# A layer's matrix products set between the small products that join the blocks of an inverse

## The chip, the cores and the metric

The kernel runs on one core of a Trainium2 chip. The metric is the device time of one execution in microseconds (us). TensorE is PE in what follows (PEld is its loading of weights), VectorE is DVE, ScalarE is ACT, GpSimd is POOL, SyncE is SP.

## The reference

A recurrence over 768 steps for 4 x 8 heads of size 40, whose output is the input of two feed-forward layers:

```python
for t in range(S):                      # S = 768, state is D x D, D = 40, for each batch and head
    y[:, :, t] = einsum('bhd,bhde->bhe', rt, state)
    Sa = einsum('bhde,bhe->bhd', state, at)
    state = state * wt[:, :, None, :] - einsum('bhd,bhe->bhde', Sa, bt) + einsum('bhd,bhe->bhde', vt, kt)
x = y.transpose(0, 2, 1, 3).reshape(3072, 320)
h = x @ w_in                            # 320 -> 1024
sm = softmax(h);  solu = h * sm         # the sum has 1e-09 added
x = layernorm(solu) * g_ln @ w_out      # 1024 -> 320
h = x @ w2_in                           # 320 -> 2048
out = (max(h, 0) + alpha * min(h, 0)) @ w2_out
```

## The kernel before

The recurrence is computed in chunks of 32 steps. There are 24 slots, `slot(g)`, one for each chunk, and 12 windows of two slots. Within a chunk the steps depend on each other through a triangular matrix of 32 x 32 for each head, whose inverse is needed. The inverses of two windows are built together, by `inverse(W)`: on DVE by 14 elimination steps for the 16 x 16 blocks, then on PE by `left` (tile pv, twice 64 matrix products) and `join` (tile pn, twice 64), which join the 16 x 16 blocks to 32 x 32. ACT copies the results (L386, L392). Each of these products is a block of 16 or 32 rows for one of four groups of partitions; `units` issues four of them for each l and then calls `pace`.

The joins for W = 1 to 5 are run in the slots 3, 7, 11, 15 and 19, at four places of the slot by `invs(0.2)`, `invs(0.4)`, `invs(0.6)` and `invs(1.0)`. The join for W = 0 is run ahead of the slots.

Within a slot PE makes, in this order: px (L437), pu (L450), pf (L473), pst (L485), pg2 (L528), pss (L505, L508) and py (L548). px needs the scans H and F of DVE (L277, L281), and py is the slot's output, multiplied by H into Yt (L552) and passed on. Before py the tile YS is copied by ACT (L535) and masked by POOL (L536).

While the recurrence runs, PE also makes the first layer for earlier chunks. For each slot `mlp_tasks` puts its work into `queue` as entries with a planned time: 16 of h (mm1, L583, one product of 128x512 each), four of ptr (tr1, L622, transposes), eight of po (mm2, L636 to L638, three products each), one of ptx (tr2, L650), and the norm (L600) and the softmax (`soft`, L588 to L597, whose power on POOL is L596). The order of PE's work is decided as the kernel is written out, by a plan of the time: `pace(dt, n)` notes the work just issued, and where the columns counted over the last 3.413 us of the plan are below a floor it calls `pop`, which issues the next entry of the queue. Where the queue is empty, `pop` issues a product whose result nobody reads: "busy" (L211) in the first slots, "zero" (L182) later, if `more()` allows it. `wait` fills planned waits the same way. Ahead of py the queue is emptied down to two entries.

The order on DVE, ACT and POOL is made by a scheduler from the same program. From about 775 us on, the second layer runs (L1022, L1040 to L1042, with L603, L604 and L1028, L1029 on the other engines).

Of the kernel before, what the change touches and what calls it, by code (L numbers as in the profile page):

```python
# [46 lines left out]
def tile_kernel(ctx: ExitStack, tc: tile.TileContext, w_fm, a0_fm, a_fm, kb_fm, r_fm, v_fm, v_tm,  # L47
# [112 lines left out]
    queue, now, seen = [], [0.0], []  # L160

    def note(dt, n):
        now[0] += dt
        seen.append((now[0] - dt, now[0], n))
        while seen[0][1] < now[0] - SPAN:
            seen.pop(0)

    def counted(ahead=0.0):
        t = now[0] + ahead - SPAN
        return sum(n * min(1.0, max(0.0, b - t) / max(b - a, 1e-6)) for a, b, n in seen)  # L170

    def pop():
        if queue:
            dt, n, f = queue.pop(0)
            f()
        elif "busy" in st:
            dt, n = 0.216, 512
            keep(1)
        else:
            dt, n = 0.216, 416  # L180
            z = ps_at.tile([128, 512], F32, name="zero", tag="at")
            nc.tensor.matmul(z, lhsT=D1[:, 1:65].bitcast(BF16), rhs=D1[:, 0:256].bitcast(BF16), start=True, stop=True)  # L182
        note(dt, n)
        return dt

    def more():
        return queue or "busy" in st or st["slot"] >= KEND and ZF[st["slot"] % 4]

    def pace(dt, n):

        note(dt, n)
        floor, extra = LEVELS[min(st["slot"] // 4, 1) if st["slot"] != 4 else 2] if st["slot"] < NG - 4 else LEVELS[3]
        if more() and counted(dt + 0.09) + n < floor:
            note(0.09, 0)
            while more() and counted() < floor + extra:
                pop()
# [12 lines left out]
    def keep(n):  # L209
        for _ in range(n):  # L210
            nc.tensor.matmul(st["busy"], lhsT=busy[:, 0:128], rhs=busy, start=True, stop=True)  # L211
# [133 lines left out]
    def inverse(W):  # L345
        X = LMN[W % 2]
        L = X[:, 0:16, :].rearrange("p t (b a) -> p b t a", b=2)
        A = LMN[2]
        box = {}

        def start():
            nc.vector.transpose(out=X[:, 15::-1, :], in_=GR[:, :, 32:48].rearrange("p l c -> p c l"))
            nc.vector.transpose(out=X[:, ::-1, 16:32].rearrange("p s c -> p c s"),
                                in_=GR[:, :, 16:32].rearrange("p l c -> p c l"))

        def step(s):
            sh = [128, 2, 15 - s, s]
            tmp = b1.tile([128, 128], F32, name="tmp")[:, 0:2 * s * (15 - s)]
            tmp = tmp.rearrange("p (b t a) -> p b t a", b=2, a=s)
            nc.vector.tensor_tensor(out=tmp, in0=L[:, :, s + 1:16, s:s + 1].to_broadcast(sh),  # L360
                                    in1=L[:, :, s:s + 1, 0:s].to_broadcast(sh), op=ALU.mult)
            o = L[:, :, s + 1:16, 0:s]
            st["step"] = nc.vector.tensor_tensor(out=o, in0=o, in1=tmp, op=ALU.add)

        def fin():
            V = b1.tile([128, 32, 16], F32, name="V", tag="Yt")
            low = tri[:, 0:256].rearrange("p (t a) -> p t a", a=16).unsqueeze(1).to_broadcast([128, 2, 16, 16])
            nc.vector.tensor_tensor(out=V.rearrange("p (b t) a -> p b t a", b=2), in0=L, in1=low, op=ALU.mult)
            nc.vector.memset(V.rearrange("p (b t) a -> p b (t a)", b=2)[:, :, ::17], 1.0)
            st["fence"] = nc.vector.transpose(out=VT.rearrange("p l a -> p a l"), in_=V.rearrange("p x a -> p a x"))  # L370
            nc.scalar.activation(out=VR[:, :, 31:15:-1], in_=VT, func=AF.Identity, scale=tri[:, 320:321])

        def units(p, lhsT, rhs, rows, ls):
            for l in ls:
                for q in range(0, 128, 32):
                    nc.tensor.matmul(p[q:q + 32, l - ls[0], :], lhsT=lhsT[q:q + rows, l, 0:32], rhs=rhs[q:q + rows, l, :],  # L376
                                     start=True, stop=True)
                pace(0.042, 16)

        def left(h):  # L380
            if h == 0:
                box["p"] = ps_at.tile([128, 32, 16], F32, name="pv", tag="at")
            p = box["p"]
            units(p[:, 16 * h:16 * h + 16], GR, VT, 16, range(16 * h, 16 * h + 16))
            if h:
                nc.scalar.copy(out=A[:, :, 0:16], in_=p)  # L386

        def join(h):
            ls = range(16 * h, 16 * h + 16)
            p = ps_at.tile([128, 16, 32], F32, name="pn", tag="at")  # L390
            units(p, A, VR, 32, ls)
            nc.scalar.copy(out=X[:, 16 * h:16 * h + 16, :], in_=p)  # L392
            st["NT", W] = X

        yield start
        for s in range(1, 15):
            yield lambda s=s: step(s)
        yield fin
        for f in (left, join):
            for h in range(2):  # L400
                yield lambda f=f, h=h: f(h)
# [396 lines left out]
    def inv_tasks(g):  # L798
        W, c4 = divmod(g, 4)
        if 2 * W + 3 >= NW or c4 < 2:  # L800
            return []
        inv = list(inverse(W + 1))
        return inv[:16] if c4 == 2 else inv[16:]
# [117 lines left out]
    def phase1():  # L921
# [19 lines left out]
        if NW > 2:  # L941
            prep_load(2)
            load_a(4)
            load_a(5)
            kb_load(2)
        inv = list(inverse(0))
        st["joins"] = inv[16:]
        for i, f in enumerate(inv[:16]):
# [416 lines left out]
```

## Time and profile before

| | |
|---|---|
| median of 3 runs | 1168.07 us |
| lowest and highest | 1164.89 and 1177.03 us |
| the profiled execution | 1169.15 us |
| its span, first to last instruction | 1167.4 us |
| mean granted clock of TensorE in it | 0.912 of full speed |
| PE busy | 1018.2 us, 87% of the span |

The profiled execution is one execution on the same core; its time is 1.75 us longer than its span. Times of the trace are counted from the span's start. Idle time of an engine is put down to what it waited for last; "issue" means that it waited for nothing that the profile shows.

### The profile page before, as it was taken

The page shows a single profiled execution, that of the slowest core. Times are in us where ns is not written, and L with a number is a line of the kernel's source. Part 1 is how long each engine was busy: PE and PEld are TensorE (multiplying, and loading weights), DVE is VectorE, ACT ScalarE, POOL GpSimd, SP SyncE. Part 2 cuts the span into 40 slices and gives each one's busy share as a digit, 9 for nine tenths or more (in the row PEclk, how much of TensorE's full clock was granted, in tenths as well). Part 3 has the DMA queues.
Part 4 walks back from the last instruction along what each step waited for, and adds up shares of the span by engine and source line. Part 5 has one row for each costly group of instructions (what it writes and reads, how often), then busy time and mean ns, then how long its engine had stood idle before and what let it go on. Part 6 is the DMA issues. An engine that isn't in the chain of part 4 may idle for free.

```text
span 1167.4 us, 43026 instructions
## 1 busy us (share of the span) xinstructions
PE 1018.2 (87%) x19030; PEld 844.2 (72%) x19030; DVE 698.0 (60%) x1382; ACT 536.1 (46%) x1222; POOL 484.2 (41%) x495
## 2 busy tenths in 40 slices
PE   7678777888887888797788889989999999999997
PEld 3455455676766776675667677778998889999997
DVE  8887876668686846584667725656534433344443
ACT  3456543666456645665565556656312121212121
POOL 6576535342353335331733233346233333333333
PEclk9799868888889967988789888999999999999999
DMA  7534343353334333342233433444401010201000
GB/s 167 142 113 113 90 129 102 81 138 101 85 92 115 104 87 94 94 126 77 64 99 92 116 107 94 117 130 143 122 4 59 10 60 10 63 6 41 6 23 15
DMA packets 104709, 100.06 MB, mean 86 GB/s; under 512 B 38084, under 2 KB 83908, under 8 KB 104516
## 3 DMA queue, kind: packets, MB, share of 16 engines
q1 hardware_dynamic: 104516, 97.24, 30.4%
q8 instruction: 151, 2.47, 0.9%
q14 instruction: 42, 0.34, 0.1%
HBM read 71.78 MB, written 25.43 MB: 83 GB/s over the span
## 4 chain that ended last, share of the span: by engine, by line
PE 49%; DVE 23%; ACT 8%; POOL 8%; issue 6%; DMA 5%; SPq 0%; POOLq 0%; DVEq 0%; ACTq 0%
PE ph L1022 15%; PE acc L1042 5%; PE acc L1040 5%; PE acc L1041 5%; PE h L583 4%; DMA kbf<-in_kb_fm_dram 3%; DVE VUS L490 2%; POOL sm L596 2%; DVE H L277 2%; DVE P L590 2%; PE busy L211 2%; DVE KBS L516 2%; DVE F L281 2%; PE pf L473 2%; PE pv L376 1%
## 5 line engine op out<-in xcount | busy, mean ns | idle before, releaser
L1029 POOL TENSOR_TENSOR gll<-gt,gh 128x512 fp32r<-128x512 f32 (+1 forms) x112 | 129.0, 1152 | 224.1 <-ACT gh L1028 223.0
L603 DVE TENSOR_SCALAR gt<-ph,al 128x512 f32<-128x512 f32 (+1 forms) x112 | 75.5, 674 | 189.7 <-PE ph L1022 189.6
L1028 ACT CAST gh<-gt 128x512 fp32r<-128x512 f32 (+1 forms) x112 | 62.5, 559 | 254.6 <-DVE gt L604 217.4
L583 PE MATMUL h<-w1h,xt 128*128 128x512 f32 x240 | 104.7, 485 | 4.4 <-ACT h L592 2.3
L536 POOL TENSOR_TENSOR YS<-YS,mask 64x512 f32<-64x512 f32 x48 | 64.3, 1340 | 84.3 <-ACT YS L535 82.6
L312 POOL TENSOR_TENSOR XS<-XS,H 40x512 f32<-40x512 f32 (+1 forms) x48 | 62.5, 1306 | 66.1 <-DMA XS<-in_a_fm_dram 32.9
L1041 PE MATMUL acc<-w2l,gh 128*128 128x320 f32 x288 | 89.0, 309 | 0.0
L1040 PE MATMUL acc<-w2h,gh 128*128 128x320 f32 x288 | 89.0, 309 | 0.0
L1042 PE MATMUL acc<-w2h,gll 128*128 128x320 f32 x288 | 88.9, 309 | 0.0
L628 DVE TENSOR_TENSOR lnl<-ptr,lnh 128x512 fp32r<-128x512 f32 x48 | 32.6, 685 | 80.3 <-ACT lnh L627 80.2
L636 PE MATMUL po<-wo1h,lnh 128*128 128x320 f32 x192 | 69.0, 359 | 8.4 <-DVE lnl L628 6.7
L211 PE MATMUL busy<-busy 128*128 128x512 bf16 x241 | 70.3, 444 | 2.3 <-POOL lims L127 1.3
L604 DVE SCALAR_TENSOR_TENSOR gt<-ph,gt 128x512 f32<-128x512 f32 (+1 forms) x112 | 68.8, 615 | 3.7
L583 PE MATMUL h<-w1l,xt 128*128 128x512 f32 x144 | 68.9, 479 | 0.0
L589 ACT ACTIVATE P<-h,sm 128x1024 f32<-128x1024 f32 x24 | 26.8, 1115 | 85.3 <-DVE sm L588 85.3
L637 PE MATMUL po<-wo1l,lnh 128*128 128x320 f32 x192 | 63.1, 329 | 2.0 <-issue 2.0
L638 PE MATMUL po<-wo1h,lnl 128*128 128x320 f32 x192 | 62.9, 328 | 0.0
L583 PEld LDWEIGHTS h<-w1h,xt 128*128 128x128 f32 x240 | 50.1, 221 | 12.8 <-ACT h L592 3.3
L1022 PE MATMUL ph<-w1h,w2h 128*128 128x512 f32 x180 | 59.3, 394 | 0.0
L336 DVE TENSOR_TENSOR XS<-pg,mask 32x256 f32<-32x256 f32 x96 | 39.8, 415 | 31.7 <-ACT GR L339 28.3
L1040 PEld LDWEIGHTS acc<-w2h,gh 128*128 128x128 f32 x288 | 54.2, 188 | 1.5
L1041 PEld LDWEIGHTS acc<-w2l,gh 128*128 128x128 f32 x288 | 54.1, 188 | 1.2
(208 smaller groups left out, 2742.0 us busy)
## 6 DMA issues: line engine op xcount, KB each, us to landing
kbf<-in_kb_fm_dram SPq DMA_DIRECT2D x24, 416.0 KB
x2d<-x SPq DMA_DIRECT2D x24, 320.0 KB
xd<-Y SPq DMA_DIRECT2D x24, 256.0 KB
xt<-xd SPq DMA_DIRECT2D x12, 512.0 KB
raw<-in_w_in_dram SPq DMA_DIRECT2D x20, 256.0 KB
wt<-in_w_fm_dram SPq DMA_DIRECT2D x24, 211.7 KB
raw<-in_w_in_dram SPq DMA_DIRECT2D x8, 512.0 KB
raw<-in_w_out_dram SPq DMA_DIRECT2D x16, 256.0 KB
```

The costliest lines, as they stand in the source:

```text
L211: nc.tensor.matmul(st["busy"], lhsT=busy[:, 0:128], rhs=busy, start=True, stop=True)
L536: nc.gpsimd.tensor_tensor(out=y[q, e], in0=y[q, e], in1=mask[q].unsqueeze(1).to_broadcast([64, 16, 32]), op=ALU.mult)
L583: nc.tensor.matmul(st["h"][:, ns], lhsT=l, rhs=r, start=j == 0, stop=j == len(ops) - 1)
L603: nc.vector.tensor_scalar(out=tmp, in0=h, scalar1=0.0, scalar2=al, op0=ALU.min, op1=ALU.mult)
L604: nc.vector.scalar_tensor_tensor(out=o, in0=h, scalar=0.0, in1=tmp, op0=ALU.max, op1=ALU.add)
L636: nc.tensor.matmul(po, lhsT=lh[:, k], rhs=wo1h[:, k], start=k == 0, stop=False)
L637: nc.tensor.matmul(po, lhsT=lh[:, k], rhs=wo1l[:, k], start=False, stop=False)
L1022: nc.tensor.matmul(p, lhsT=l, rhs=r, start=j == 0, stop=j == len(ops) - 1)
L1029: nc.gpsimd.tensor_tensor(out=gll, in0=t, in1=f32(gh), op=ALU.subtract)
L1040: nc.tensor.matmul(acc, lhsT=gh[:, cs], rhs=oh, start=f == 0, stop=False)
L1041: nc.tensor.matmul(acc, lhsT=gh[:, cs], rhs=ol, start=False, stop=False)
L1042: nc.tensor.matmul(acc, lhsT=gll[:, cs], rhs=oh, start=False, stop=f == K2 - 1)
```

## The change

In `units`, after every fourth l (that is after 16 small products) one entry of the queue is issued, if the queue holds any. Nothing else is edited. Lines of the kernel from L379 on have a number two higher afterwards.

```diff
@@ -376,6 +376,8 @@
                     nc.tensor.matmul(p[q:q + 32, l - ls[0], :], lhsT=lhsT[q:q + rows, l, 0:32], rhs=rhs[q:q + rows, l, :],
                                      start=True, stop=True)
                 pace(0.042, 16)
+                if queue and l % 4 == 3:
+                    pop()
 
         def left(h):
             if h == 0:
```

On PE, the first `left` of slot 11 and what follows it, before (pu and pv are of the recurrence and the inverse, h and ptr of the layer, pf of the recurrence again):

```order
L450 MATMUL pu<-XP,LMN_160 32x40 x32
L376 MATMUL pv<-VT,GR 32x16 x64
L459 LDWEIGHTS D_148
L459 MATMUL pf<-D_148 32x256
L473 MATMUL pf<-LMN_160,XP 40x32 x4
L583 MATMUL h<-w1h,xt 128x512
L583 MATMUL h<-w1l,xt 128x512
L583 MATMUL h<-w1h,xt 128x512
L622 MATMUL ptr<-ident,P 128x128 x2
```

The same place of PE after the change:

```order
L452 MATMUL pu<-XP,LMN_160 32x40 x32
L376 MATMUL pv<-VT,GR 32x16 x16
L585 MATMUL h<-w1h,xt 128x512
L376 MATMUL pv<-VT,GR 32x16 x16
L585 MATMUL h<-w1l,xt 128x512
L376 MATMUL pv<-VT,GR 32x16 x16
L585 MATMUL h<-w1h,xt 128x512
L376 MATMUL pv<-VT,GR 32x16 x16
L624 MATMUL ptr<-ident,P 128x128 x2
L461 LDWEIGHTS D_148
L461 MATMUL pf<-D_148 32x256
L475 MATMUL pf<-LMN_160,XP 40x32 x6
```

Three products of h and the first pair of ptr now stand between the four parts of pv, and no longer behind the first products of pf. The second `left` (pv) of the slot takes in two pairs of ptr and two products of h in the same way, and the two `join` (pn) take in seven of the eight groups of po.

The end of slot 11 on PE before, from the second join to the next slot's px:

```order
L376 MATMUL pn<-VR,LMN_162 32x32 x64
L505 MATMUL pss<-ident,VUS_167 40x40 x26
L636 MATMUL po<-wo1h,lnh 128x320
...
L638 MATMUL po<-wo1h,lnl 128x320
L182 LDWEIGHTS D_148
L182 MATMUL zero<-D_148 128x512
L505 MATMUL pss<-ident,VUS_167 40x40 x6
L459 LDWEIGHTS D_148
L459 MATMUL py<-D_148 32x512
L548 MATMUL py<-YS_172,KBS_158 40x32 x32
L437 MATMUL px<-VUS_167,XS_150 32x40 x32
```

The same after the change:

```order
L376 MATMUL pn<-VR,LMN_162 32x32 x16
L507 MATMUL pss<-ident,VUS_167 40x40 x32
L461 LDWEIGHTS D_148
L461 MATMUL py<-D_148 32x512
L550 MATMUL py<-YS_172,KBS_158 40x32 x28
L182 LDWEIGHTS D_148
L182 MATMUL zero<-D_148 128x512
...
L182 MATMUL zero<-D_148 128x512
L550 MATMUL py<-YS_172,KBS_158 40x32 x4
L439 MATMUL px<-VUS_167,XS_150 32x40 x32
```

The po that stood between the pss products are gone from there, the one zero too, and six zeros, of which the first and the last are shown, stand within py. The same holds for slots 7, 15 and 19. In slot 3 the queue is used up in the two `left`; its two `join` have nothing set between. In all there are 39 zeros where there were 19, and 242 busy products where there were 241; every other product is there as often as before.

On DVE in slot 7, the order around the sum L595 that the power L596 on POOL takes, before (wc, F, rs, kbf and H prepare the next windows, em is a step in decoding weights):

```order
L594 TENSOR_SCALAR sm<-sm 128x1
L273 TENSOR_SCALAR wc<-wt 104x8x64
L274 MEMSET wc 104x9
L281 SCALAR_TENSOR_TENSOR F<-wc,D_148 104x520
L664 TENSOR_SCALAR em_5405<-raw_5404 128x256
L595 TENSOR_SCALAR sm<-sm 128x1
L286 RECIPROCAL Dx<-F 104x8
L291 TENSOR_TENSOR rs<-H,F 104x8
L303 TENSOR_TENSOR kbf<-kbf,F 104x16x32
L277 SCALAR_TENSOR_TENSOR H<-wc,Dx 104x520
```

The same on DVE after the change:

```order
L596 TENSOR_SCALAR sm<-sm 128x1
L273 TENSOR_SCALAR wc<-wt 104x8x64
L274 MEMSET wc 104x9
L666 TENSOR_SCALAR em_5416<-raw_5415 128x256
L281 SCALAR_TENSOR_TENSOR F<-wc,D_148 104x520
L667 TENSOR_SCALAR em_5416<-raw_5415 128x256
L597 TENSOR_SCALAR sm<-sm 128x1
L286 RECIPROCAL Dx<-F 104x8
L291 TENSOR_TENSOR rs<-H,F 104x8
L303 TENSOR_TENSOR kbf<-kbf,F 104x16x32
L277 SCALAR_TENSOR_TENSOR H<-wc,Dx 104x520
```

The two first decoding steps (L664 and L665, now L666 and L667) come ahead of the scan F and of the sum. In slots 11 and 15 they stood in this order already, before the change and after it.

## Rows read from the trace of the kernel before

**Rows 1.** The page: busy time and instructions; instruction queue; chain that ended last.

```profile
PE 1018.2 (87%) x19030; PEld 844.2 (72%) x19030; DVE 698.0 (60%) x1382; ACT 536.1 (46%) x1222; POOL 484.2 (41%) x495
...
q8 instruction: 151, 2.47, 0.9%
...
PE 49%; DVE 23%; ACT 8%; POOL 8%; issue 6%; DMA 5%; SPq 0%; POOLq 0%; DVEq 0%; ACTq 0%
```

**Rows 2.** Waits of PE: total us, times, longest us.

```profile
PE pv L376 <- issue: 13.3, 6, 2.8
...
PE pn L376 <- issue: 10.8, 5, 4.4
```

**Rows 3.** Windows, five slots: us, PE, PEld, DVE, ACT, POOL, clock, DMA.

```profile
157.00:197.80 40.80, 34.28 (x1009) 24.09 (x1008) 30.67 (x53) 17.62 (x40) 16.55 (x15) 0.71 0.40 117
280.10:319.90 39.80, 32.16 (x1024) 26.88 (x1023) 26.17 (x62) 24.57 (x56) 12.81 (x15) 0.79 0.26 69
402.30:448.00 45.70, 36.55 (x1025) 29.52 (x1023) 22.84 (x58) 23.50 (x56) 19.26 (x17) 0.66 0.25 63
528.40:574.30 45.90, 32.06 (x1024) 26.09 (x1023) 22.12 (x55) 22.70 (x52) 19.26 (x17) 0.77 0.25 63
654.00:692.90 38.90, 29.39 (x1024) 24.28 (x1023) 15.92 (x43) 24.55 (x56) 10.22 (x13) 0.87 0.35 103
```

**Rows 4.** Timeline of PE: start, us, what, [idle before].

```profile
293.22 0.37 PE L376 MATMUL pv<-VT,GR 16*32 16x16 f32 x21 [1.64 <-issue]
...
413.15 0.72 PE L376 MATMUL pv<-VT,GR 16*32 16x16 f32 x37 [1.18 <-issue]
...
538.77 0.63 PE L376 MATMUL pv<-VT,GR 16*32 16x16 f32 x53 [2.59 <-issue]
...
548.67 0.23 PE L376 MATMUL pv<-VT,GR 16*32 16x16 f32 x1 [2.58 <-issue]
...
666.53 0.44 PE L622 MATMUL ptr<-ident,P 128*128 128x128 f32 x2 [0.54 <-ACT P L600]
...
673.21 0.41 PE L376 MATMUL pv<-VT,GR 16*32 16x16 f32 x16 [2.75 <-issue]
...
687.54 0.56 PE L376 MATMUL pn<-VR,LMN 32*32 32x32 f32 x41 [0.97 <-issue]
```

**Rows 5.** Timeline of PE, end of slot 11.

```profile
443.87 0.58 PE L182 MATMUL zero<-D 104*128 104x512 bf16 x1 [3.94 <-ACT YS L535]
```

**Rows 6.** Chain of waits, slot 11: start, us, what.

```profile
433.41 7.47 POOL sm L596
...
441.18 1.24 ACT P L600
...
445.55 2.57 PE py L548 x64
```

**Rows 7.** Timeline of POOL: slot 7's power, slot 11's masks.

```profile
310.72 1.02 POOL L596 TENSOR_TENSOR sm<-sm,half 128x1 f32<-128x1 f32 x1 [1.58 <-DVE rs L291]
...
443.13 2.59 POOL L536 TENSOR_TENSOR YS<-YS,mask 64x512 f32<-64x512 f32 x2 [1.99 <-ACT YS L535]
```

**Rows 8.** Chain of waits, slot 15: full clock, half clock.

```profile
542.94 0.46 PE h L583 x2
...
550.08 0.43 PE h L583
```

**Rows 9.** Windows, slots 11, 11, 15 (columns as in rows 3).

```profile
411.90:427.10 15.20, 14.02 (x289) 11.14 (x287) 2.77 (x4) 5.62 (x12) 0.00 (x0) 0.51 0.45 119
437.30:448.00 10.70, 6.76 (x87) 5.37 (x87) 3.49 (x9) 5.18 (x11) 8.33 (x7) 0.50 0.09 31
546.00:553.40 7.40, 4.82 (x57) 3.81 (x48) 1.81 (x2) 1.18 (x2) 0.00 (x0) 0.54 0.09 29
```

**Rows 10.** End of slot 7: timeline of PE, then chain of waits.

```profile
318.56 1.42 PE L548 MATMUL py<-YS,KBS 104*40 104x32 f32 x64
...
320.08 1.17 issue
```

## The prediction

> **What bounds the kernel now.** I read the page first. TensorE (PE) is busy for 87% of the span with 19,030 matrix products and 19,030 weight loads, and the chain that ended last is half PE and a quarter VectorE (DVE) [rows 1]. So a change in PE's order can matter, but only in the stretch where it stands. The edit stands inside `units`, the 16 small products for each four l of `left` (tile pv) and `join` (tile pn). It acts only where the queue holds entries at that point: the joins of slots 3, 7, 11, 15 and 19. The first join, ahead of the slots, finds an empty queue. The second layer, after some 775 us, has no joins.
>
> Next the waits of PE. The largest wait there is PE standing at pv for nothing that the profile shows ("issue"): 13.3 us in 6 places, and 10.8 us in 5 places at pn [rows 2]. Those 24.1 us lie in the lines that the edit touches, so they are the most that this edit could remove by filling stalls.
>
> Then the five slots by themselves: 40.8, 39.8, 45.7, 45.9 and 38.9 us, 211.1 us together, with a granted clock of 0.71, 0.79, 0.66, 0.77 and 0.87 [rows 3]. The time of these slots has three parts that the edit can reach: the stalls, the half clock, and what PE does at the slot's end.
>
> Which stalls are on the path? I followed the chain of waits in each slot. In slots 7, 11 and 15 it runs through PE up to the last product of h, then leaves PE: DVE and ScalarE (ACT) make the layer's softmax, GpSimd (POOL) makes the power of L596, ACT makes the normalisation L600, and the copies of YS stand behind that on ACT. In slot 11 the power takes 7.47 us and L600 1.24 us before PE gets on [rows 6]. PE arrives early and waits 3.94 us for it [rows 5]. So time saved at a pv block, ahead of the last h, counts, and a stall at a pn block of these slots counts nothing: PE would only wait longer. Slot 19 is the exception: its power is short and PE itself reaches py last there, so its stall of 0.97 us at pn [rows 4] is on the path.
>
> **The change part by part.** *The pv stalls.* On the path they are 1.64 us in slot 7, 1.18 in slot 11, 2.59 and 2.58 in slot 15 and 2.75 in slot 19 [rows 4]. Why does PE stop there? Products and loads make 38,060 instructions and the instruction queue q8 with the larger count brought 151 packets [rows 1], about 252 of PE's instructions to a packet if all are PE's. In slot 15, 53 small products and as many loads pass in 0.63 us, so a packet's worth passes in 1.5 us [rows 4]. A product of h is one instruction pair that lasts 0.23 us at full clock and about 0.43 at half [rows 8]. I take it, from this, that PE runs out of instructions in the small products and that a layer product put ahead of the stall shortens it by its own length, no more. (An argument from sums; no row shows it directly.)
>
> In slot 7 three products of h now come before the end of the first block: 3 x 0.23 to 3 x 0.43 = 0.7 to 1.3; I take 1.0 of the 1.64. In slot 11 the stall comes with 37 of the block's records still behind it, so two to three products come ahead of it: 0.5 to 1.18; I take 1.0. In slot 15 the first stall has one or two products ahead of it, 0.2 to 0.9, and the second comes at the block's last product, with an h and two pairs of ptr ahead of it, 0.7 to 1.3; I take 0.4 + 0.9 = 1.3. In slot 19 the stall of 2.75 would lose as much, 0.7 to 1.3, and its pn stall up to 0.97, but there PE reaches the transposes ptr of P sooner. It waits for L600 there already, 0.54 us [rows 4]; the pf products that stood ahead of it are now behind, so some 0.6 us come back. I take +0.4. Slot 3: its queue is used up in the pv blocks, the pn blocks have nothing put between, and the longest stall at pn, 4.4 us [rows 2], is its own; I take 0, within +-1.5. Sum: **3.7 us gained**, between 1.5 and 7.
>
> Interposing costs nothing in itself: the entries are not new, they come out of bursts that stood further down. The h and ptr that leave the pst burst, and the po that leave the pg and pss bursts, are taken off there.
>
> *What stands at the end.* The queue is emptied earlier, so the pacer, which fills with zero products when the queue is dry, has nothing else left in py. In slots 7, 11, 15 and 19 the one zero before the last pss products goes, and six zeros stand in a row after 28 of the 32 py pairs. The old zero of slots 7, 11 and 15 came out of a wait and ran while POOL's mask was still under way, so it was free. The new ones stand between py and everything that follows: Yt, px of the next slot, its scans. py itself can't begin earlier to make room, because it waits for the mask on POOL: in slot 11 that ends at 443.13 + 2.59 = 445.72, py begins at 445.55 and needs both halves [rows 6, 7].
> Price of one zero: the nearest row at full clock is h, 0.23; at half clock 0.43 [rows 8]. Slots 11 and 15 end at half clock, 0.50 in their last 10.7 us [rows 9]: 6 x 0.43 = 2.6 us each. Slot 7 is at full clock there (py in 1.42 against 2.57 us [rows 6, 10]): 6 x 0.23 = 1.4, but the chain at its end is DVE's, and Yt stands at 1.17 us of "issue" after py [rows 10], so between 0.2 and 1.4; I take 0.8. Slot 19: a zero was on PE's path already, so 5 x 0.23 = 1.1. Sum: 2.6 + 2.6 + 0.8 + 1.1 = **7.1 us lost**, between 4.3 (all at full clock, slot 7 hidden: 1.4 + 1.4 + 0.4 + 1.1) and 8.9 (all at half but slot 19's).
>
> *The clock.* In slots 7, 15 and 19 a stretch at half clock begins just after a stall: in slot 15 the second one, 546.0 to 553.4, has 4.82 us of PE work at 0.54 [rows 9]. Where a shorter stall leaves the clock up, half of such a stretch's PE work comes back, 2.4 us. Slot 11 enters its first block at half clock already and has 14.02 us of PE work at 0.51 [rows 9], so up to 7 us could come back, but the layer products that raised it at 427 come in one burst today, and spread among small products each of them stands alone; it may as well come up later. I take about one such stretch spared of the four slots: **2 us gained**, between 4 lost (two such stretches more) and 14 gained (7 in slot 11, three of 2.4 in the others).
>
> *Other engines.* The DVE and ACT orders shift a little around the joins. The one place that matters is the power L596: 7.47 us in slots 11 and 15, 1.02 in slot 7 [rows 6, 7]. In slot 7 DVE's order now is the same as in slots 11 and 15 (L665, a step of a weight's decoding, ahead of L595). If L596 is long there too, py of slot 7 goes from 318.56 to where slot 11's stands after the power's start, 445.55 - 433.41 = 12.1 us after 310.72, that is 322.9: 4.3 us. In slots 11 and 15 the reverse can happen: then PE's 3.94 us wait is what there is to gain in each. I take 0 for both.
>
> **Sum:** -3.7 + 7.1 - 2.0 = +1.4 us on the execution's own 1169.15 us (span 1167.4 and 1.75 around it). That execution is 1.1 us above the median of 1168.07, so the forecast on the median is 1169.5 us: no difference that can be measured. Runs of this kernel lie between 1164.89 and 1177.03, and 1% (11.7 us) is about what a measurement can tell from no change.
>
> By the Trainium skill's page "Runtime: NRT & Kernel Launch", section "Instruction fetch mechanics", PE's instructions are fetched ahead in blocks of 256 and the fetch is hidden by the pace at which they are issued; by that rule the pv stalls would not be the fetch's, and what is put among them would give back nothing of it. The sum without the stalls' term would be +5.1 us. The trace speaks against "hidden": 24.1 us of issue waits stand in just the lines with the most instructions per microsecond [rows 2].
>
> **The rivals.**
> *It gets clearly faster.* The stalls go entirely, not by the length of what is put between, and the clock stays up: 1.64 + 1.18 + 5.17 + 2.75 = 10.7 us of stalls, and with the clock up in the blocks 6 to 10 us more, against 4.3 for the zeros: -12 to -16, so 1152 to 1156. For it: half-clock stretches follow stalls. Against it: the same number of instructions has to come through in the same order, and slot 11 is at half clock before its block. Chance 0.13.
> *It gets slower.* The pacer's zeros at half clock, with the power of slot 7 grown long and no clock gained: 8.9 for the zeros + 4.3 for slot 7 + up to 4 for a clock that comes up later in slots 11 and 15, less 2 of stalls: +11 to +15, so 1179 to 1183. It decides at the place of L596 in slot 7: it needs that to be over 5 us. For it: DVE's order there is now that of the two slots where it is long. Against it: in slot 7 the same scans ran beside it already and it took 1.02. Chance 0.17.
> *It does nothing.* The stalls only move to the next small products (pst, pg), since the fetch is what is short, and the zeros fall into waits further on: within 2 us of 1168. Chance 0.2, the same side as the forecast.
> The forecast itself, a loss and a gain of a few us each: 0.5.
>
> **How the numbers follow.** Within 1%: 0.5 + 0.2 = 0.70; faster 0.13, slower 0.17. Without the clock the bounds of the terms go from -7 + 4.3 = -2.7 to -1.5 + 8.9 + 4.3 = +11.7. The clock's gains reach 14 below, and of these I take in 9, so the range begins at 1168 - 2.7 - 9 = 1156; above, 11.7 and some 1.5 of the clock's loss end it at 1181. It leaves out the far half of each outer rival, 0.15 together.
>
> **What would show it.** In the changed kernel: "issue" at pv falls from 13.3 to about 9 us; slots 11 and 15 keep a long L596 and a wait of PE just before py instead of at the zero; six zeros of about 0.43 us inside py in slots 11 and 15, with Yt later by as much; L596 of slot 7 near 1 us. I am wrong if the granted clock of slot 11 or 15 moves by more than 0.1, if L596 changes its length in any of the slots, or if the stalls vanish altogether.

## The result and the profile after

The changed kernel takes 1183.42 us, median of 12 runs (1177.15 to 1193.07), against 1167.87 us of the kernel before beside it: the ratio is 1.0127, with an interval of 1.0093 to 1.016. That is slower by over 1%, and above the end of my range, 1181. The profiled execution has a span of 1180.1 us, 12.7 more than before.

The page of the changed kernel (busy time of the engines; the row for [rows 1]) and its waits of PE ([rows 2]: total, times, longest):

```profile
PE 1040.9 (88%) x19051; PEld 847.5 (72%) x19051; DVE 703.7 (60%) x1382; ACT 535.7 (45%) x1222; POOL 487.0 (41%) x495
```

```profile
PE pv L376 <- issue: 5.8, 5, 2.1
...
PE pn L376 <- issue: 4.2, 4, 2.6
```

PE's stalls at pv and pn fell from 24.1 to 10.0 us, and still the kernel is slower: PE's busy time rose from 1018.2 to 1040.9 us. The stalls were filled, with work that takes longer. The five slots with joins, in windows (columns as in [rows 3]):

```profile
158.00:201.00 43.00, 35.92 (x1010) 24.97 (x1009) 28.73 (x49) 15.32 (x34) 14.90 (x13) 0.69 0.39 112
287.70:335.60 47.90, 40.17 (x1029) 29.65 (x1028) 27.08 (x63) 24.35 (x56) 17.39 (x17) 0.71 0.26 64
415.90:461.90 46.00, 38.55 (x1029) 28.12 (x1028) 24.75 (x55) 22.73 (x53) 17.40 (x17) 0.78 0.27 65
541.70:587.80 46.10, 38.92 (x1033) 27.64 (x1032) 24.72 (x55) 22.59 (x53) 17.86 (x17) 0.74 0.28 71
663.70:704.40 40.70, 34.17 (x1029) 25.51 (x1028) 16.47 (x43) 24.53 (x56) 10.51 (x13) 0.87 0.34 98
```

Against [rows 3] the slots 3, 7, 11, 15 and 19 took 2.2, 8.1, 0.3, 0.2 and 1.8 us more. Of the slots without a join one is longer by much: slot 5, from its first px to the next slot's, took 32.2 us in place of 28.1. The others moved by 2.9 us or less.

Why slot 7? The stretch that counts there runs from the first pv to the last h, since the softmax hangs on that product. First the kernel before, slots 7, 11, 15 and 19 (columns as in [rows 3]), then the changed one:

```profile
290.25:303.50 13.25, 11.59 (x370) 9.48 (x361) 1.82 (x4) 6.39 (x14) 0.72 (x1) 0.76 0.43 121
410.51:425.93 15.42, 14.24 (x369) 11.65 (x358) 2.02 (x4) 6.97 (x16) 0.44 (x1) 0.50 0.51 133
535.34:552.21 16.87, 11.70 (x374) 9.46 (x363) 2.02 (x4) 7.41 (x18) 0.91 (x1) 0.72 0.45 122
663.33:676.93 13.60, 10.31 (x375) 8.32 (x363) 2.02 (x4) 7.14 (x17) 0.73 (x1) 0.84 0.59 188
```

```profile
297.58:314.03 16.45, 15.77 (x379) 11.05 (x367) 2.09 (x4) 6.58 (x15) 0.69 (x1) 0.59 0.48 125
422.92:440.30 17.38, 15.93 (x378) 11.13 (x366) 2.09 (x4) 7.39 (x18) 0.92 (x1) 0.61 0.45 118
548.71:566.04 17.33, 16.69 (x378) 11.55 (x365) 2.09 (x4) 7.39 (x18) 0.92 (x1) 0.53 0.45 118
673.56:687.12 13.56, 12.34 (x379) 8.77 (x367) 2.09 (x4) 7.10 (x17) 0.66 (x1) 0.84 0.60 189
```

Read the length, PE's busy time and the clock in each row. Before, the stretches are 13.25, 15.42, 16.87 and 13.60 us long, and the difference to PE's busy time, its idle time, is 1.7, 1.2, 5.2 and 3.3 us. After, the idle time is 0.7, 1.4, 0.6 and 1.2 us: 7.3 us less in all. But PE's work for the same products is 60.7 us in place of 47.8. Together the four stretches are 5.6 us longer, 64.7 in place of 59.1. The clock fell in slots 7 and 15, from 0.76 and 0.72 to 0.59 and 0.53; in slot 11 it rose from 0.50 to 0.61, and in slot 19 it stayed at 0.84.

Two more rows of the changed kernel: the six zeros in slot 7 in the chain of waits (start, us), and the power on POOL in slots 7 and 11 (answering to [rows 7] and [rows 6]):

```profile
333.35 2.08 PE zero L182 x6
```

```profile
321.73 4.53 POOL L598 TENSOR_TENSOR sm<-sm,half 128x1 f32<-128x1 f32 x1 [1.75 <-DVE rs L291]
...
448.00 4.52 POOL L598 TENSOR_TENSOR sm<-sm,half 128x1 f32<-128x1 f32 x1 [1.75 <-DVE rs L291]
```

The zeros take 2.08 us on the path in slot 7, and in the same way 2.09 in slot 11 and 2.51 in slot 15. The power takes 4.53 us in slot 7, where it took 1.02, and 4.52 in slots 11 and 15, where it took 7.48 and 7.49.

### The profile page after: what moved, and what is told of

It is laid out like the page before. It is cut to its first block, busy times and chain, and to the rows that moved or that the text cites. A ratio compares the mean times of both kernels' runs of the same rounds, so it can differ in the third digit from the quotient of the medians.

```text
span 1180.1 us, 43067 instructions
## 1 busy us (share of the span) xinstructions
PE 1040.9 (88%) x19051; PEld 847.5 (72%) x19051; DVE 703.7 (60%) x1382; ACT 535.7 (45%) x1222; POOL 487.0 (41%) x495
## 4 chain that ended last, share of the span: by engine, by line
PE 54%; DVE 19%; ACT 9%; POOL 6%; issue 6%; DMA 5%; SPq 0%; POOLq 0%; DVEq 0%; ACTq 0%
PE ph L1024 15%; PE h L585 6%; PE acc L1044 5%; PE acc L1043 5%; PE acc L1042 5%; PE pf L475 2%; DVE F L281 2%; PE pst L487 2%; PE ptr L624 2%; DMA kbf<-in_kb_fm_dram 2%; DVE P L592 2%; PE pv L376 2%; DVE VUS L492 1%; PE py L550 1%; PE po L638 1%
## 5 line engine op out<-in xcount | busy, mean ns | idle before, releaser
L312 POOL TENSOR_TENSOR XS<-XS,H 40x512 f32<-40x512 f32 (+1 forms) x48 | 65.8, 1375 | 72.7 <-DMA XS<-in_a_fm_dram 34.1
L492 DVE TENSOR_TENSOR VUS<-pst,VUS 40x320 f32<-40x320 f32 x92 | 44.9, 488 | 21.2 <-PE pst L487 19.1
```

Source lines behind the costliest of these rows:

```text
L312: (nc.vector if w < 2 and e in DA else nc.gpsimd).tensor_tensor(out=o, in0=o, in1=h, op=ALU.mult)
```

## The experiments

Each was timed against the kernel before on the same chip; ratios are to that kernel, with their intervals. The stretches, slot lengths and clocks are from one profiled execution each.

**Which part costs?** Three kernels undo one part each, a fourth leaves out slot 3. The first has no zeros in slots 7, 11, 15 and 19:

```diff
-ZF = (1, 1, 1, 1)
+ZF = (1, 1, 1, 0)
```

> The changed kernel, without any zero product in the slots 7, 11, 15 and 19 (the six in py, and none in their place); nothing else of the order on TensorE moves in them. Three theories. Zeros: the loss of some 15 us is above all the 24 zeros in py, which took 2.08, 2.15, 2.58 us in slots 7, 11 and 15: without them the time is 1174 to 1176. Switches: a layer product set alone among small products costs 0.43 instead of 0.23 us at full clock and 0.72 instead of 0.43 at half, and keeps the clock at half: without the zeros 1176 to 1180, and slot 7 still takes over 44 us. Side effects: the loss is the longer power on GpSimd in slot 7 and the later kbf load in slot 5: 1178 to 1183.

Measured: 1.009 [1.0059, 1.0122], 1178.49 us. The zeros' part is 1.0127 - 1.009, some 4 us, which is not clear of the two intervals; the rest of the loss stays, with slot 7 at 44.0 us. The zeros are not all of it.

Interposing in `left` alone, and in `join` alone:

```diff
-                if queue and l % 4 == 3:
+                if rows == 16 and queue and l % 4 == 3:     # left alone; rows == 32: join alone
```

> Layer products are set between the products of left (pv) alone; join (pn) as before. No zeros in py, none in slots 7, 11, 15, 19 at all. Zeros theory: as the kernel before, 1165 to 1169. Switch theory: the last h comes later by 2.8 us in slot 7 and 0.6 to 0.8 in slots 11 and 15, so 4 to 9 us above the kernel before, 1172 to 1177, with the granted clock at 0.5 to 0.6 from the second pv block to the last h. Side effects: slot 7's power stays above 4 us, slot 5 stays at 32 us, 1174 to 1178.

Measured: 1.0128 [1.008, 1.0176], 1183.3 us, the whole loss without a zero in these slots, and more than any of the three theories gave it. The theory that the zeros are nearly all of it falls here. The power is another one in this run too, 7.48 us in slots 7, 11 and 15 where the changed kernel has 4.52, so what the zeros are worth doesn't follow from it.

> Layer products are set between the products of join (pn) alone; left (pv) as before; the six zeros stand in py. Zeros theory: 6 to 8 us above the kernel before, 1174 to 1176. Switch theory: the joins lie in the time in which TensorE waits for the power on GpSimd, so the switches there cost nothing in slots 11 and 15 and the rest is the zeros: 1172 to 1176. Side effects: slot 3 has nothing set between here, so slot 5 is back at 28 us; 1168 to 1172 if slot 7's power is short.

Measured: 0.9995 [0.9973, 1.0018], 1167.73 us, no difference, with all the zeros in py. In slots 11 and 15 the power took 4.52 us in place of 7.48, which pays for the zeros: those slots took 42.9 and 44.4 us in place of 45.7 and 45.9, though each has six zeros.

```diff
-                if queue and l % 4 == 3:
+                if st["slot"] > 3 and queue and l % 4 == 3:
```

> The change in slots 7, 11, 15 and 19 alone; slot 3 as before. Side effects: slots 3 to 6 are as in the kernel before (the slots 3 to 5 took 7 us more in the changed kernel), so 1176 to 1178. Switch and zeros theories: slot 3 has four switches and no zeros in py, so 0.5 to 2 us are given back: 1181 to 1183.

Measured: 1.0105 [1.0063, 1.0148], 1181.59 us. Slot 5 is back at 28.3 us, but the interval is too wide to say what slot 3's part is worth. Inconclusive, and so the next asks the other way round.

**Slot 3 alone, and the joins without the zeros.**

```diff
+                if rows == 16 and st["slot"] == 3 and queue and l % 4 == 3:
```

> Layer products between the products of left in slot 3 alone; everything else as the kernel before. Theory A: slot 5 takes 32 us where the kernel before takes 28, since its kbf load starts later (the orders on VectorE and ScalarE are moved); slot 3 gives back nothing or a little, so 1170 to 1173. Rival B (slot 5 of the changed kernel was long for some other reason, as the state of the clock): 1166 to 1169, and slot 5 at 26 to 29 us.

Measured: 1.0038 [1.0017, 1.0059], 1174.84 us, and slot 5 at 32.6 us. In all six programs with single entries in `left` of slot 3 and the load as it was, slot 5 took 31.6 to 32.6 us; in the ten with `left` of slot 3 and the load as they were, 26.1 to 30.8. Why is it late? SyncE's own timeline (start, us, what is asked for), the kernel before and then this one, with the load in the chain of waits of this one below:

```profile
237.21 0.56 SPq L230 DMA_DIRECT2D kbf<-in_kb_fm_dram  x1
240.52 0.36 SPq L724 DMA_DIRECT2D wd<-dec  x1
240.93 0.39 SPq L230 DMA_DIRECT2D kbf<-in_kb_fm_dram  x1
```

```profile
244.55 0.35 SPq L726 DMA_DIRECT2D wd<-dec  x1
245.00 1.04 SPq L230 DMA_DIRECT2D kbf<-in_kb_fm_dram  x2
```

```profile
245.69 6.20 DMA kbf<-in_kb_fm_dram
```

In the kernel before, the first half of kbf is asked for at 237.21, 6.0 us into the slot (which begins at 231.2), ahead of the store of decoded weights (wd), and the second half behind it. With the change in slot 3, both halves stand behind the store, at 245.00, which is 10.4 us into the slot (234.6), and the load takes 6.20 us. The store waits for POOL's dec, and that for a decoding step (em) on ScalarE that stands behind a row of copies of KBS in the chain of waits. The change moved no load; it moved the order that the scheduler made of the queue.

> Layer products between the products of join alone, and no zeros in slots 7, 11, 15 and 19. Theory A (the joins' part shortens the power on GpSimd from 7.48 to 4.52 us in slots 11 and 15, and the zeros of 2 to 2.6 us eat that): without the zeros 4 to 8 us below the kernel before, 1160 to 1164, with slots 11 and 15 near 41 us. Rival B (the zeros warm the clock for the next slot, so that they pay for themselves): 1167 to 1170, with slots 8, 12, 16 longer by 1 to 2 us each.

Measured: 0.9966 [0.9936, 0.9996], 1165.02 us. Without zeros, the joins' part is a small gain: slots 7, 11 and 15 took 39.0, 40.3 and 43.5 us. Theory A's direction, at the weak end of its size, and above the time that it gave.

**The power left out**, in both kernels (a multiplication on VectorE stands in its place, so the output is another one):

```diff
-        nc.gpsimd.tensor_tensor(out=col(8), in0=col(7), in1=half, op=ALU.pow)
-        nc.gpsimd.tensor_tensor(out=col(9), in0=col(8), in1=col(3), op=ALU.mult)
+        nc.vector.tensor_tensor(out=col(8), in0=col(7), in1=half, op=ALU.mult)
+        nc.vector.tensor_tensor(out=col(9), in0=col(8), in1=col(3), op=ALU.mult)
```

> The changed kernel, with the power of the layer's normalisation left out: the two small operations of L596 and L597 stand on VectorE, and a multiplication takes the place of the power. Theory A: the power's 4.5 us in slots 7, 11 and 15 fall to 1 to 2, so 2.5 to 3.5 us less in each, and slot 7 ends near 44 us: 1172 to 1177. Rival B (the power is hidden behind TensorE's own longer work): 1180 to 1184.

> The kernel before, with the power left out in the same way. Theory A: slots 11 and 15, where it takes 7.48 us and TensorE waits 3.9 us for what follows it, give back 3.5 to 5.5 us each, slot 7 nothing: 1157 to 1162. The difference to the changed kernel without the power is then what the interposed products cost by themselves, 12 to 18 us. Rival B: 1166 to 1169.

Measured: 0.9979 [0.9952, 1.0007] and 0.9912 [0.989, 0.9934], 1169.78 and 1160.65 us. The changed kernel gains more than I expected, the other as expected. The difference between the two is 9.1 us, less than the 12 to 18 that I expected, against 15.5 with the power. So most of the loss, some 9 us, doesn't go by way of the power. The other 6 are hardly clear of the noise (0.60% by the ratios, with 0.5% either way), and how they come about I can't show: the change makes the power longer in slot 7 but shorter in slots 11 and 15, and the three together fell from 16.0 to 13.6 us.

**Slot 5, slot 7 and the later slots, each by itself.** The first asks for kbf at the end of slot 4, beside `left` in slot 3:

```diff
+                if W == 1:
+                    add('z', lambda: kb_load(u))
...
-                add(LD, lambda: kb_load(u), lambda: load_a(2 * u + 1))
+                add(LD, *([lambda: kb_load(u)] if W != 1 else []), lambda: load_a(2 * u + 1))
```

> As the run with layer products in the left of slot 3 alone, and the load of kbf for slot 5 asked for at the end of slot 4, so that on SyncE it stands ahead of the store of decoded weights (wd) behind which the change had moved it. Theory A (slot 5 is late because SyncE's queue lets the load wait for that store): slot 5 back to 26 to 28.5 us, the time 1167 to 1171. Rival B (slot 5 is late for the order on ScalarE or VectorE, the load only follows): slot 5 still 31 to 32.5, 1172 to 1176.

Measured: 1.0001 [0.998, 1.0023], 1169.15 us, slot 5 at 25.8 us. The loss of 0.38% is gone. Its SyncE has the load ahead of the store again:

```profile
235.56 0.74 SPq L230 DMA_DIRECT2D kbf<-in_kb_fm_dram  x2
240.48 0.35 SPq L726 DMA_DIRECT2D wd<-dec  x1
```

Then `left` in slot 7 alone (`st["slot"] == 7` in the condition):

> Layer products between the products of left in slot 7 alone. Theory A: the power in slot 7 takes 4.5 to 7.5 us in place of 1.0, since the order on VectorE is then that of slots 11 and 15; with a last h 1 to 2.5 us later slot 7 is 45 to 48 us, the whole 1173 to 1178. Rival B (the power's length comes from the interposed joins or from slot 3): the power stays at 1 us, 1168 to 1171.

Measured: 1.0033 [1.0008, 1.0058], 1174.9 us; slot 7 took 48.5 us, with its power at 7.48 and its last h 26.2 us into the slot in place of 23.4.

Then `left` in slots 11, 15 and 19 alone (`st["slot"] > 7`):

> Layer products between the products of left in slots 11, 15 and 19 alone; slots 3 to 7 as before. Here the orders on the other engines hardly move, so this is what interposing costs on TensorE by itself. Theory A (each one among small products costs 0.2 to 0.3 us more than in a burst and keeps the clock at half): the last h comes 0.5 to 1.5 us later in each, 1170 to 1173. Rival B (as I predicted: the stalls give back 1 us or more in each): 1164 to 1167.

Measured: 1.0049 [1.0028, 1.0069], 1176.73 us, more than either theory said. The stretch from the first pv to the last h in the three slots, and two rows of PE's timeline in slot 11:

```profile
412.56:429.96 17.40, 17.27 (x373) 11.99 (x362) 2.09 (x4) 6.96 (x16) 0.45 (x1) 0.50 0.44 118
541.38:558.75 17.37, 17.32 (x373) 11.98 (x362) 2.09 (x4) 6.96 (x16) 0.43 (x1) 0.50 0.46 118
668.98:683.96 14.98, 14.98 (x372) 10.65 (x362) 1.89 (x4) 6.38 (x14) 0.00 (x0) 0.61 0.54 171
```

```profile
413.84 0.62 PE L376 MATMUL pv<-VT,GR 16*32 16x16 f32 x32
414.39 0.80 PE L585 MATMUL h<-w1l,xt 128*128 128x512 f32 x1
415.12 0.98 PE L376 MATMUL pv<-VT,GR 16*32 16x16 f32 x32
```

PE has no idle time left there, 0.13, 0.05 and 0.00 us, and 17.3, 17.3 and 15.0 us of work in place of 14.2, 11.7 and 10.3. Slot 11 shows what the changes between kinds of product cost, since its clock is 0.50 in both kernels: 3.0 us. The two rows show where: from h at 414.39 to the next pv at 415.12 it is 0.73 us, where one h after another is 0.43 [rows 8]. In slot 19 of the changed kernel, at the upper level of the clock, it is 0.43 us, where one h after another is 0.23 [rows 8]:

```profile
673.95 0.50 PE L585 MATMUL h<-w1h,xt 128*128 128x512 f32 x1
674.38 0.44 PE L376 MATMUL pv<-VT,GR 16*32 16x16 f32 x32
```

In slots 15 and 19 of the run with the later slots alone, the clock was 0.50 in place of 0.72 and 0.61 in place of 0.84 besides. The mean clock of whole executions was lower too: 0.908 in the 12 of this run, 0.913 in the 35 of the kernel before beside them, with some 0.003 either way on the difference.

The three parts, 0.38, 0.33 and 0.49%, add up to 1.20%, with some 0.4% either way, and `left` in all five slots cost 1.28%, with 0.48%.

**Pairs: half of the changes.** Two entries after every 32 products, in `left` alone:

```diff
-                if queue and l % 4 == 3:
-                    pop()
+                if rows == 16 and queue and l % 8 == 7:
+                    pop()
+                    pop()
```

> Left alone in all five slots, but two entries after every 32 small products in place of one after every 16: the same work is moved, with half of the changes between kinds of product. If the changes are what delays the last h, it comes 0.8 to 1.2 us sooner in slots 7, 11, 15 and 19 than in the run with left alone, 3 to 5 us less in all: 1177 to 1180. If the half clock is, the same as that run: 1181 to 1185. If slot 5 and slot 7's power are nearly all of it, also 1181 to 1185, and the last h no later than in the kernel before.

Measured: 1.0041 [1.0015, 1.0066], 1173.92 us, less than I had said. The last h came 15.8, 16.7, 17.8 and 15.3 us after the first pv with single entries, and 14.8, 15.2, 17.6 and 14.5 with pairs, 3.5 us less in all. The power was at 4.52 in slots 7, 11 and 15 too, so this run alone does not tell the causes apart. Nor is the cost of slot 3 gone: slot 5 was at 25.7 us, but slot 4 took 40.1 in place of 33.4. Another load, that of VUS, stands behind the store there, and the chain of waits runs through it:

```profile
236.35 0.33 SPq L727 DMA_DIRECT2D wd<-dec  x1
236.77 0.85 SPq L428 DMA_DIRECT2D VUS<-in_v_tm_dram  x2
```

Hence the last, pairs in slots 11, 15 and 19 alone (`st["slot"] > 7` added):

> Left in slots 11, 15 and 19 alone, two entries after every 32 products; to be held against the run with one entry after every 16 in the same slots, where TensorE had no idle time left from the first pv to the last h in slots 15 and 19 (0.05 and 0.00 us, in place of 5.2 and 3.3) but 17.3 and 15.0 us of work in place of 11.7 and 10.3, at a clock of 0.50 and 0.61 in place of 0.72 and 0.84. If the clock is the cause and follows from how thinly the layer products lie: with pairs the clock is 0.6 or more and the work under 15.5 and 13.5 us. If the changes between kinds of product are the cause: half of the extra work goes at the same clock, 14.5 and 12.7 us. Time 1168 to 1174 in either case, 1175 or more in neither.

Measured: 0.9905 [0.9884, 0.9927], 1161.86 us, faster than the kernel before by nearly 1%, and below the 1168 that was the lowest time I had given it. Its three stretches:

```profile
411.80:427.51 15.71, 14.49 (x371) 10.80 (x362) 2.09 (x4) 6.95 (x16) 0.43 (x1) 0.61 0.50 130
534.83:550.30 15.47, 14.50 (x373) 10.79 (x364) 2.09 (x4) 6.98 (x16) 0.48 (x1) 0.61 0.51 133
657.47:672.17 14.70, 11.00 (x372) 8.37 (x362) 1.91 (x4) 6.40 (x14) 0.01 (x1) 0.85 0.55 174
```

14.5, 14.5 and 11.0 us of work at a clock of 0.61, 0.61 and 0.85: both bounds that I had set for the clock are met. But the gain is not in these stretches, which are 45.9 us long together, as in the kernel before. Slots 11 to 18 took 244.5 us in place of 251.7, and what is seen to differ there is the power, at 4.52 us in slots 11 and 15 in place of 7.48; that it is the whole gain is not shown.

Slot 19 gives the price of the changes by itself, since three programs have nearly the same clock there: 10.31 us of work at 0.84 in the kernel before, 12.34 at 0.84 in the changed kernel, 11.0 at 0.85 with pairs. So all the changes cost 2.0 us and half of them 0.7. With the clock at 0.61 the single entries cost 4.7.

How far is the clock of one execution to be trusted? From the first pv to the last h PE's order is the same in all programs that leave `left` of a slot alone, and the same in all with single entries there, so the other traces answer that. Means of PE's work and idle time in us, and the lowest and highest clock:

| slot | `left` | programs | work | idle | clock |
|---|---|---|---|---|---|
| 7 | as before | 12 | 12.5 | 1.9 | 0.59 to 0.82 |
| 7 | single entries | 7 | 14.6 | 0.7 | 0.59 to 0.84 |
| 11 | as before | 11 | 12.4 | 2.9 | 0.50 to 0.77 |
| 11 | single entries | 7 | 16.2 | 0.8 | 0.50 to 0.63 |
| 15 | as before | 11 | 12.3 | 4.0 | 0.59 to 0.73 |
| 15 | single entries | 7 | 16.6 | 0.6 | 0.50 to 0.59 |
| 19 | as before | 11 | 10.3 | 3.4 | 0.74 to 0.85 |
| 19 | single entries | 7 | 13.9 | 0.8 | 0.61 to 0.84 |

In every slot the single entries have more work and less idle time, and the four stretches are 4.7 us longer in sum. In slot 15 the clock is 0.59 or less with single entries and 0.59 or more without. But in slot 7 both orders got 0.59 and over 0.8, and in slot 19 the single entries got 0.61 four times and 0.83 or 0.84 three times. So the order within the stretch does not settle the clock by itself; what else does, no run here shows.

**What holds the power.** The product behind it is put on VectorE, so that VectorE waits for the power:

```diff
-        nc.gpsimd.tensor_tensor(out=col(9), in0=col(8), in1=col(3), op=ALU.mult)
+        nc.vector.tensor_tensor(out=col(9), in0=col(8), in1=col(3), op=ALU.mult)
```

> The changed kernel, with the product that follows the power (L597 before, L599 now) on VectorE in place of GpSimd; the power itself stays on GpSimd. VectorE has to wait for the power there, so its run of instructions is broken soon after the power begins. Theory A (the power lasts until VectorE has nothing to issue): the power in slots 7, 11 and 15 falls from 4.5 to under 2.5 us, and the time by 5 to 12 us, to 1171 to 1178. Rival B (the power's length has nothing to do with VectorE's run): it stays at 4.5, the time at 1181 to 1185.

> The kernel before with the same edit and nothing else. Theory A: the power in slots 11 and 15 falls from 7.48 to under 2.5 us; up to the 3.9 us that TensorE waits there are given back in each: 1159 to 1164. Rival B: 7.48 us as before, 1167 to 1171.

Measured: 1.0118 [1.0089, 1.0146] and 1.0043 [1.0022, 1.0064], 1186.45 and 1175.69 us. Half of theory A holds. The power fell to 1.02 us in slots 11 and 15 of both and in slot 7 of the changed one (1.02 before already in the other), with VectorE's order ahead of it as it was. In slot 11 of the kernel before, it ended at 440.88, and VectorE's first pause after it had begun was between these two instructions, at 440.37:

```profile
439.72 0.65 DVE L303 TENSOR_TENSOR kbf<-kbf,F 104x512 f32<-104x512 f32 x1
440.43 0.41 DVE L273 TENSOR_SCALAR wc<-wt 104x512 f32<-104x512 f32 x1
```

With the product on VectorE, the power and VectorE's wait for it are:

```profile
438.69 1.02 POOL L596 TENSOR_TENSOR sm<-sm,half 128x1 f32<-128x1 f32 x1 [1.75 <-DVE rs L291]
```

```profile
439.74 1.21 DVE L597 TENSOR_TENSOR sm<-sm 128x1 f32<-128x1 f32 x1 [0.45 <-POOL sm L596]
```

But the time did not fall. In the kernel before with this edit, slots 8, 12 and 16 took 34.4, 33.2 and 33.6 us in place of 32.3, 31.2 and 31.2. That needn't be the edit's price: slots 12 and 16 took 34.1 and 33.7 us in the run of the joins without zeros too, where the product stands on GpSimd and slots 11 and 15 are shorter. What is longer only with the product on VectorE is the time from the first px of slot 23 to the end: 412.1 to 415.4 us in the four programs that have it there behind a power, 409.6 to 411.3 in the fourteen that don't. VectorE now has to wait for each of the 24 powers; that this is the price I take from the edit, I did not follow it. My sum counted the gain in two slots and no price in the others.

> Layer products among the products of join alone, no zeros in slots 7, 11, 15 and 19, and the product after the power on VectorE. Theory A: the joins' part has its gain from the shorter power, so on top of the edit on VectorE it adds nothing or up to 3 us: 1157 to 1164, as the kernel before with that edit. Rival B (the joins' part gains by filling stalls in the joins): 4 us or more below that kernel.

Measured: 1.0048 [1.0022, 1.0075], 1176.01 us, the same as the kernel before with that edit: with the power short in both, the joins' part adds nothing. Its gain was the power, as theory A said, though the time is far above the 1157 to 1164 that it gave.

> As the run before it, and the load of kbf for slot 5 asked for at the end of slot 4. Slot 5 was 2.4 us shorter with the early load than in the kernel before, but the slots around it moved too: 1155 to 1163.

Measured: 1.0013 [0.9987, 1.0038], 1170.95 us; a miss, the product on VectorE costs more than the early load gives.

**A version that beats both**: the joins' part, no zeros, the early load, and the product left on GpSimd.

> Layer products among the products of join alone, no zeros in slots 7, 11, 15 and 19, the power's product on GpSimd as it was, and the load of kbf for slot 5 asked for at the end of slot 4. The two edits that gave something by themselves: 4 us for the joins without zeros, up to 2 in slot 5. Expected 1161 to 1166; if the early load only shifts the wait, 1164 to 1168.

Measured: 0.9842 [0.9818, 0.9865], 1154.73 us, 17 us less than the kernel before, below the 1161 to 1166 expected and more than the two parts by themselves. (The early load was run only together with other edits, not by itself on the kernel before.) The power has become short in every slot (instruction xcount: shortest, median, longest ns):

```profile
L598 POOL TENSOR_TENSOR sm<-sm,half x24: 543/549/1020, 204.1 to 811.0; 128x1 f32<-128x1 f32 x24
```

In this program VectorE's order in slots 11 and 15 is that which slot 7 had before: one decoding step behind the scan F and ahead of the sum, in place of one on each side of the scan. In all fourteen programs in which power and product stand on GpSimd, at the three places (slots 7, 11 and 15), 42 in all, it is so: with one step between the scan and the sum and none ahead of the scan the power takes 1.0 us (10 places), with one on each side 4.5 (18) or 7.5 (14). Each of the 32 long ones ended 0.35 to 0.53 us after VectorE's first pause. Where that pause, of 0.05 to 0.07 us, comes late, as above, the power takes 7.5; where VectorE runs out of work after the second scan F, it takes 4.5, as in slot 11 of the changed kernel, whose power began at 448.00 and ended at 452.52:

```profile
450.95 1.23 DVE L281 TENSOR_TENSOR_SCAN F<-wc,D 104x520 f32<-104x520 f32 x1
455.94 0.42 DVE L672 SCALAR_TENSOR_TENSOR em<-raw,em 128x256 f32<-128x256 uint32 x1 [3.77 <-ACT em L669]
```

## Why the prediction was wrong

*What bounds the kernel, and where the edit acts.* Right: the five slots with joins, the stalls at pv, the path through the last h and the power. Stalls at the joins indeed counted nothing: with the power short, 1.0043 without and 1.0048 with products among them.

*The pv stalls, 3.7 us gained.* Right in place, too small in size: PE's idle time from the first pv to the last h fell by 7.3 us, and all of its "issue" at pv from 13.3 to 5.8, not to about 9; in the run with slots 11, 15 and 19 alone the idle time fell to next to nothing. That a layer product shortens a stall by its own length and no more did not hold. That PE runs out of instructions there was argued from sums, and no run shows it: of the eleven stalls at pv and pn in the kernel before, eight have a packet of q8 in them or within 1 us ahead, three have none, and packets some 5 us apart, as they come in these slots, would meet six or seven by chance.

*"Interposing costs nothing in itself."* This step failed. The h and the ptr are the same, but each stands alone among small products, and such an h takes 0.73 us in place of 0.43 at half clock, 0.43 in place of 0.23 at full. In one stretch that is 2.0 us in slot 19 at an unchanged clock of 0.84 and, in the run with the later slots alone, 3.0 in slot 11 at an unchanged 0.50.

*The clock, 2 us gained.* This failed too. I took the half clock for something that follows a stall. In slots 15 and 19 of the run with the later slots alone the stalls were gone, and the clock was lower, 0.50 and 0.61 where it had been 0.72 and 0.84, with PE at work the whole stretch. In the changed kernel's execution it fell in two of the four stretches and rose in one. Whole executions with single entries in the later slots had a mean of 0.908 in place of 0.913, so there the clock lost and did not gain; what decides the clock of a stretch stays open. Together with the step before it, PE's work in the four stretches is 12.9 us longer, against 7.3 us of idle time taken away.

*The zeros, 7.1 us lost.* Right in place. In slots 11 and 15 the size was near, 2.09 and 2.51 us for 2.6 each; in slot 7 it was 2.08 for 0.8. What they cost the whole is less clear: some 4 us by the run without them (1.0127 to 1.009) and 3 to 4 by the joins with and without (0.9995 to 0.9966), neither clear of its intervals.

*Other engines, 0.* This failed. The power of slot 7 became 4.53 us, as the slower rival had it, though under the 5 us that I named as its turning point; `left` in slot 7 alone cost 0.33%. In slots 11 and 15 the reverse came, 7.48 to 4.52, which the prediction named and put at nothing. And slot 5, which I did not look at, lost 4 us through SyncE's queue; `left` in slot 3 alone cost 0.38%. The order of SyncE was to be had before the run, and its waits in the kernel before show it waiting for POOL's dec; I read the orders of the engines in the slots with joins and stopped there.

So the loss of 1.27% is: `left` in slot 3 by way of slot 5's load, 0.38%; `left` in slot 7 with the power, 0.33%; `left` in the later slots on TensorE itself, 0.49%; and the joins' part with the zeros about 0, a shorter power against the zeros. The slower rival's 1179 to 1183 nearly met the time, and that was luck in good part: it had the power of slot 7 and a loss by the clock, but neither the load of slot 5, nor the price of the changes, nor the shorter power in slots 11 and 15. Of the three signs of being wrong that I named, two came: the clock of slot 11 went from 0.66 to 0.78, and the power changed its length in three slots.

What stays open: why one decoding step more ahead of the sum makes the power last until VectorE's next pause, and with one fewer not, while the first four instructions on VectorE behind it are the same. In slot 7 of the kernel before, VectorE went on without a pause, and the power ended 0.41 us after the product kbf beside which it had begun. By the Trainium skill's page "Advanced Engine Details and Errata", section "Mode Summary", VectorE's second port to the memory SBUF is shared with GpSimd, so that GpSimd's instructions and those of VectorE that run in a mode with two ports block each other. The trace agrees with a block, 7.48 us against 1.02; which instruction of VectorE holds it, and whether it runs in such a mode, no run here shows.

## What to carry to other kernels

A stall that is filled is worth only what the filling costs in its new place: compare the engine's busy time over the same stretch, not its idle time, before and after. Layer products set singly among small ones cost more than in pairs: 2.0 against 0.7 us in slot 19 at nearly the same clock. When an order on one engine is changed in a scheduled program, read the orders of all queues for two slots further on, that of the queue which asks for loads first.

## What was not expected of the hardware

TensorE at work without a pause for 17.3 us was granted a clock of 0.50, where the same products with 5.2 us of pauses had 0.72 (slot 15; over all traces 0.50 to 0.59 against 0.59 to 0.73). In slots 7, 11 and 15 a power of 128 numbers on GpSimd takes 1.02 us or up to 7.5, until VectorE's next pause, and which of them goes with the place of two decoding steps of some 0.3 us on VectorE.
